# Turning attention outputs and q by DMA transposes instead of by TensorE, in a fused attention and gated-convolution kernel

## The chip, the cores and the metric

One core of a Trainium2 chip. The time is that of one execution on the device, in microseconds, as the median of several executions. "Span" is the stretch from the first to the last instruction in the profiled execution; it is 1.6 to 1.9 us shorter than the time. An execution is called slow when it is over 1.5% above the fastest of its kernel. Slices of a profile are counted from 0.

## The reference, cut to what matters

Block attention whose keys and values are first mixed by a small matrix P per head (five rounds of row and column normalisation), then two dense layers with a depthwise convolution as gate between them. There are 4 batches, 8 heads, 768 positions, head size 64; blocks of 96 positions; model width 512, inner width 1024.

```python
k_sorted = np.einsum('bhij,bhjcd->bhicd', P, k_b)     # v_sorted alike
scores = scale * np.matmul(q_b, k_sb.transpose(0, 1, 2, 4, 3))
attn = softmax(scores);  o = np.matmul(attn, v_sb)
x = o.transpose(0, 2, 1, 3).reshape(B, S, H * D)
h = np.maximum(x @ w_in, 0.0)
out = (h * sigmoid(conv3(h, conv_w))) @ w_out
```

The kernel's matmuls sum over the partitions of both operands (the first dimension of a tile), so q must lie as (head dim, position) before the scores, and the attention output as (model width, position) before the first dense layer. Both have to be transposed, in pieces of 64 or 128 columns. That is what the change is about.

## The kernel before

All work is cut into tokens such as `T.1.3d2` (step T, batch 1, part 3, PSUM slot d2). A long table gives their order, and each engine executes its share of that order, in order. The letters: Q turns q, K and V mix keys and values, S scores, E exponentials, PV attention times values, X normalisation, T turns the output, H first dense layer, C convolution, O second dense layer; a trailing `e` is the copy out of PSUM. Loads (`lk`, `lq`, `lv`, `wout`) are issued by GpSimd, stores by SP.

```python
def turn_q(b, g, slot):                       # 24 transposes: 4 heads of one batch
    ps = psum.tile([128, 2, 1024], BF, name=slot)
    ...
                nc.tensor.transpose(ps[hh * 64:(hh + 1) * 64, e, x * 128:(x + 1) * 128],
                                    qb[b][:, h, x * D:(x + 1) * D], ident, tile_position=(0, hh * 64))

def do_T(b, j, eng, slot):                    # 4 transposes of 96x128
    xn = at.pop(("X", b, j))
    ps = bank(slot, [128, 4, BLK], BF)
    for ii in range(4):
        nc.tensor.transpose(ps[:, ii, :], xn[:, ii].rearrange("c h d -> c (h d)"), ident[0:BLK, 0:BLK])
    at[("T", b, j)] = ps

def do_Te(b, j, eng, slot):                   # copy to SBUF, permuted to position order
    ...
    copy_to(eng, xT[(b, s)][:, hp].rearrange("p (x i t) -> p x i t", x=NX, i=4),
            at.pop(("T", b, j)).rearrange("p i (x t) -> p x i t", x=NX))
```

The softmax here doesn't subtract the row's maximum and nothing guards it: scores larger than these inputs give would overflow.

## Time and profile before

| | before |
|---|---|
| time, median of 3 | 178.76 us (178.65 to 184.08) |
| TensorE busy | 162.9 us of 176.1 |
| VectorE (DVE), ScalarE (ACT) busy | 118.4 and 116.7 us |
| granted TensorE clock | 0.999 |
| input loads under way | until about 64 us |

The prediction below shows and reads the page.

### The profile page before, as it was taken

The numbers are of one execution on the slowest core, as the hardware profiler recorded it, in microseconds if no ns is written. First come the engines' busy times: TensorE is split into PE (matmuls) and PEld (weight loads), VectorE is DVE, ScalarE is ACT, GpSimd is POOL, SyncE is SP. The second block draws the span as 40 slices with busy tenths as digits, with TensorE's granted clock in tenths as the row PEclk, the third lists the DMA queues.
The fourth block names the chain that finished last, engine by engine and source line by source line (L and its number), as shares of the span: only waits on it lengthen the run. The fifth ranks groups of instructions, "written<-read, shape, count | busy, mean of one in ns | idle before, by whom it ended". The sixth has DMA issues, their size and how long they took to land.

```text
span 176.1 us, 6511 instructions
## 1 busy us (share of the span) xinstructions
PE 162.9 (92%) x2907; PEld 106.9 (61%) x2918; DVE 118.4 (67%) x224; ACT 116.7 (66%) x210; POOL 42.0 (24%) x96
## 2 busy tenths in 40 slices
PE   3997989998889999999999999999999999999991
...
DMA  3994799999999960000113322110001000131443
GB/s 48 200 212 89 113 219 217 196 220 209 215 200 218 203 110 4 0 7 0 63 60 120 121 92 90 62 61 4 2 4 60 6 0 0 63 119 60 180 181 119
DMA packets 10688, 18.27 MB, mean 104 GB/s; under 512 B 908, under 2 KB 6052, under 8 KB 10660
## 3 DMA queue, kind: packets, MB, share of 16 engines
...
## 4 chain that ended last, share of the span: by engine, by line
PE 69%; ACT 13%; DVE 10%; issue 3%; DMA 3%; DVEq 0%; ACTq 0%
PE D L502 22%; PE D L447 22%; PE D L467 9%; ACT et L402 4%; PE D L413 4%; PE D L333 3%; PE D L367 3%; DVE hE L457 3%; PE D L430 2%; ACT kT L102 2%; ACT hE L455 2%; DMA sn<-in_sort_net_dram 2%; PE D L394 2%; PE D L230 2%; ACT sg L486 2%
## 5 line engine op out<-in xcount | busy, mean ns | idle before, releaser
L447 PE MATMUL D<-xT,w_in_bf 128*128 128x384 bf16 x256 | 46.3, 326 | 0.8 <-DVE hE L457 0.5
L502 PE MATMUL D<-w_out_bf,hg 128*128 128x512 bf16 x181 | 42.7, 379 | 0.6 <-issue 0.2
L447 PEld LDWEIGHTS <-w_in_bf 128*128 128x128 bf16 x256 | 23.6, 98 | 15.4 <-issue 1.3
L495 DVE SCALAR_TENSOR_TENSOR hg<-sg,hE 128x768 bf16<-128x768 bf16 x32 | 30.8, 981 | 2.7 <-ACT sg L486 2.5
L486 ACT ACTIVATE sg<-D 64x384 bf16<-64x384 f32 x64 | 31.1, 486 | 0.8
L502 PEld LDWEIGHTS <-hg 128*128 128x128 bf16 x192 | 17.8, 98 | 20.6 <-issue 0.8
L354 POOL COPY rv<-vr 128x384 bf16<-128x384 bf16 x24 | 20.9, 910 | 36.6 <-PE D L367 25.6
L402 ACT ACTIVATE et<-D 128x768 bf16<-128x768 f32 x32 | 24.3, 820 | 6.6 <-PE D L394 6.6
L457 DVE TENSOR_SCALAR hE<-D 128x384 bf16<-128x384 f32 x29 | 15.7, 554 | 16.2 <-ACT hE L455 9.7
L455 ACT ACTIVATE hE<-D 128x384 bf16<-128x384 f32 x35 | 16.1, 491 | 14.6 <-PE D L447 7.7
L422 DVE TENSOR_TENSOR xn<-D,rc 96x512 bf16<-96x512 f32 x32 | 22.0, 687 | 1.1
L467 PE MATMUL D<-hE,dg 64*64 64x384 bf16 (+2 forms) x512 | 19.6, 286 | 0.7 <-PE D L394 0.5
L484 ACT ACTIVATE sg<-D 128x384 bf16<-128x384 f32 x32 | 15.8, 492 | 4.2 <-PE D L467 3.4
L106 DVE COPY o_sb<-D 128x512 f32<-128x512 f32 x13 | 8.9, 692 | 13.6 <-PE D L502 11.0
L467 PEld LDWEIGHTS <-dg 64*64 64x64 bf16 x512 | 12.5, 106 | 6.6 <-issue 3.6
L102 ACT COPY o_sb<-D 128x512 f32<-128x512 f32 x11 | 6.4, 587 | 13.8 <-PE D L502 13.7
L413 PE MATMUL D<-vE,et 128*128 128x65 bf16 x256 | 13.2, 194 | 0.8 <-ACT hE L455 0.5
L413 PEld LDWEIGHTS <-et 128*128 128x128 bf16 x256 | 10.6, 98 | 4.2 <-issue 2.2
L102 ACT CAST kT<-D 128x1024 bf16<-128x1024 f32 x10 | 9.9, 1013 | 3.5 <-PE D L333 3.3
L394 PE MATMUL D<-qT,kT 64*128 64x96 bf16 x256 | 9.5, 204 | 1.2 <-DVE qT L106 0.3
L420 DVE RECIPROCAL rc<-D 96x8 f32<-96x8 f32 x32 | 6.3, 198 | 6.0 <-PE D L413 5.9
L430 PE MATMUL D<-ident,xn 96*128 96x96 bf16 x128 | 9.9, 206 | 0.3
...
## 6 DMA issues: line engine op xcount, KB each, us to landing
...
qb<-in_q_dram POOLq DMA_DIRECT2D x3, 768.0 KB, 18.5
...
sn<-in_sort_net_dram SPq DMA_DIRECT2D x1, 8.0 KB, 3.2
```

The lines of the kernel that those rows point to most:

```text
L102: nc.scalar.copy(dst, src)
L354: nc.gpsimd.tensor_copy(rv[:, n * 8:(n + 1) * 8, 0:CC], vr[b].rearrange("p c d -> p d c")[:, n * 8:(n + 1) * 8, :])
L402: nc.scalar.activation(et[:, 0:8 * BLK].rearrange("c (h q) -> c h q", h=2), at.pop(("S", b, j))[:, :, 0:4 * BLK], AF.Exp, scale=scale)
L413: nc.tensor.matmul(pov[:, hh, ii, :], lhsT=et[:, o:o + 128], rhs=vE[b % 2][:, (hh * HP + hp) * NB + sub * 4 + ii, 0:65], start=True, stop= ...
L422: nc.vector.tensor_mul(xn.rearrange("c i h d -> c h i d"), pov[0:BLK, :, :, 0:64], rc.unsqueeze(3).to_broadcast((BLK, 2, 4, D)))
L447: nc.tensor.matmul(ph[:, n, 0:384], lhsT=w_in_bf[:, kc, f * 128:(f + 1) * 128], rhs=xT[(b, s)][:, kc, :], start=(kc == 0), stop=(kc == KC ...
L455: nc.scalar.activation(hv, src, AF.Relu, scale=0.5)
L457: nc.vector.tensor_scalar(hv, in0=src, scalar1=0.0, scalar2=0.5, op0=OP.max, op1=OP.mult)
L467: nc.tensor.matmul(pu[o:o + 64, n, (x0 - 3 * n) * 128:(x0 - 3 * n + nx) * 128], lhsT=dg[64 * i:64 * (i + 1), tap, f, :], rhs=src[64 * i:64 ...
L486: nc.scalar.activation(sg[o:o + 64, 384:768], pu[64 - o:128 - o, 1, 0:384], AF.Tanh)
L495: nc.vector.scalar_tensor_tensor(out=hg.rearrange("p (x c) -> p x c", c=128), in0=sg.rearrange("p (x c) -> p x c", c=128), scalar=1.0, in1 ...
L502: nc.tensor.matmul(po, lhsT=hgs[(b, f)][:, x * 128:(x + 1) * 128], rhs=w_out_bf[:, f, :], start=(f == 0), stop=(f == FC - 1))
```

## The change

The intent: take 192 of the transposes, and the copies behind them, off TensorE, ACT and DVE, and let the DMA crossbar write the turned data straight into SBUF. The outputs of batches 1 to 3 (24 transposes of 96x512, token `T.b.js`) and q of batches 2 and 3 (4 transposes of 128x1536, token `Q.b.gs`, after a copy `Qc` on DVE that puts head pairs side by side) are issued by SP. The order table is a new one (not repeated here). The cut below, with gaps marked, also leaves out the new layouts of q and of the turned outputs in SBUF.

```diff
-NET, NHE, NSG, NXN, NOS = 6, 12, 6, 4, 6
+NET, NHE, NSG, NXN, NOS = 6, 12, 6, 8, 6
 ...
-        qb[b] = rows.tile([128, H, NX * D], BF, name="qb")
+        qb[b] = rows.tile([128, H, NX * D], BF, name="qb", bufs=1)
 ...
 def do_Q(b, g, eng, slot):
-    at[("Q", b, g)] = turn_q(b, g, slot)
+    if b < 2:
+        at[("Q", b, g)] = turn_q(b, g, slot)
+        return
+    qTs[(b, g)] = att.tile([128, NX, 2, 128], BF, name=f"qT{(2 * b + g) % 4}", bufs=1)
+    nc.sync.dma_start(out=qTs[(b, g)].rearrange("p x e t -> p (x e) t"), in_=at.pop(("Qc", b, g)), transpose=True)
+def do_Qc(b, g, eng, slot):
+    qp = rows.tile([128, NX, 4, D], BF, name="qp")
+    nc.vector.tensor_copy(qp, qb[b][:, 4 * g:4 * g + 4].rearrange("p h (x d) -> p x h d", d=D))
 ...
 def do_T(b, j, eng, slot):
     xn = at.pop(("X", b, j))
+    if eng == "S":
+        nc.sync.dma_start(out=xt_part(b, j), in_=xn.rearrange("c i h d -> c (i h d)"), transpose=True)
+        return
 ...
 def do_H(b, p, s, eng, slot):
-                             rhs=xT[(b, s)][:, kc, :], ...
+                             rhs=xT[(b, s)][:, kc].rearrange("p i (x t) -> p x i t", t=PB), ...
```

More of the change, by code (lines that the diff above doesn't have):

```diff
@@ L13 @@
 AX = mybir.AxisListType
-NET, NHE, NSG, NXN, NOS = 6, 12, 6, 4, 6
+NET, NHE, NSG, NXN, NOS = 6, 12, 6, 8, 6
 SUBS = [(hp, s) for s in range(2) for hp in range(4)]
 ORDER = """
-Q.0.1d0 K.0.2d1 K.0.1d2 Qe.0.1d Ke.0.2a M.0.2d1 M.0.1d0 win.0 M.0.0d3 Ke.0.1d lk.1 bdm.0d2 Me.0.2a Me.0.0a K.0.0d1
-lv.1 lq.1 lk.2 Ke.0.0a Me.0.1d lv.2 bdv.0 V.0.0d0 V.0.1d2 S.0.0d3 S.0.1d1 dg.0.2 Ve.0.0d E.0.0 Ve.0.1d V.0.3d0
-S.0.2d2 E.0.1 V.0.2d3 E.0.2 S.0.3d1 Ve.0.3d S.0.5d0 bd.1 Ve.0.2d bd.3 E.0.3 PV.0.0d3 X.0.0 E.0.5 S.0.6d2 PV.0.1d1
@@ L24 @@
-S.0.7d0 X.0.1 PV.0.2d3 lq.2 E.0.6 T.0.0d2 S.0.4d1 E.0.7 Te.0.0a PV.0.3d0 E.0.4 X.0.2 T.0.1d3 bd.2 PV.0.5d2 Te.0.1a
-T.0.2d1 X.0.3 Te.0.2d T.0.3d0 Te.0.3d PV.0.4d3 X.0.5 PV.0.6d1 H.0.0.0d0 R.1.7 H.0.2.0d2 X.0.4 K.1.1d3 He.0.1.0a
-He.0.0.0d He.0.5.0d He.0.4.0a K.1.2d0 Ke.1.2a X.0.6 Ke.1.1d K.1.0d2 H.0.3.0d1 lk.3 T.0.4d3 Ke.1.0a R.1.1 R.1.6
-T.0.5d0 Te.0.4d PV.0.7d2 R.1.0 He.0.7.0d H.0.1.0d3 He.0.6.0a R.1.2 R.1.3 X.0.7 dg.0.1 T.0.6d1 Te.0.5d He.0.2.0a
-He.0.3.0d Te.0.6d V.1.3d2 V.1.0d0 Ve.1.0a Q.1.1d1 Ve.1.3d Q.1.0d3 lq.3 R.1.5 T.0.7d0 Qe.1.1d Te.0.7a S.1.3d1 Qe.1.0d
@@ L29 @@
-E.1.3 S.1.2d2 dg.0.0 S.1.0d3 E.1.2 S.1.1d0 H.0.2.1d1 S.1.5d2 E.1.1 V.1.1d0 R.1.4 E.1.0 He.0.5.1d He.0.4.1d E.1.5
-Ve.1.1d S.1.4d3 C.0.5d1 V.1.2d2 R.2.1 E.1.4 K.2.1d0 Ce.0.5 Ve.1.2d H.0.1.1d3 R.2.7 PV.1.3d2 Ge.0.5 PV.1.1d1 Ke.2.1a
-X.1.3 He.0.2.1a R.2.0 X.1.1 C.0.2d0 R.2.3 He.0.3.1a H.0.0.1d3 PV.1.0d1 Ce.0.2 T.1.3d2 He.0.0.1d X.1.0 He.0.1.1a
-S.1.7d0 PV.1.2d3 Te.1.3a C.0.1d2 E.1.7 T.1.0d1 Ce.0.1 PV.1.7d0 Te.1.0a X.1.2 H.0.3.1d3 X.1.7 He.0.7.1d He.0.6.1a
-T.1.2d0 Te.1.2d S.1.6d2 E.1.6 Ge.0.1 C.0.3d1 T.1.1d3 PV.1.5d0 Q.2.0d2 Te.1.1a X.1.5 R.2.2 R.2.6 K.2.2d3 Ce.0.3
@@ L34 @@
-Ke.2.2a Q.2.1d0 Qe.2.0d C.0.0d1 C.0.7d2 PV.1.6d3 Qe.2.1d Ce.0.0 H.1.0.0d0 X.1.6 Ce.0.7 T.1.7d1 Te.1.7a H.1.1.0d3
-He.1.0.0d Q.3.1d2 Q.3.0d1 Ge.0.2 He.1.2.0a He.1.3.0a Ge.0.3 He.1.1.0a Qe.3.1d K.2.0d3 T.1.6d0 R.2.5 Ge.0.0 Ke.2.0a
-lv.3 R.2.4 H.1.3.0d2 He.1.7.0a PV.1.4d3 He.1.6.0a Te.1.6d V.2.2d0 Qe.3.0d C.0.4d1 T.1.5d2 X.1.4 H.1.2.0d3 Ve.2.2d
-Ce.0.4 T.1.4d0 Te.1.5d S.2.1d2 C.0.6d1 He.1.4.0d He.1.5.0a S.2.3d3 E.2.1 Te.1.4d K.3.1d0 Ge.0.7 Ce.0.6 E.2.3 wout.0
-H.1.2.1d2 Ke.3.1d S.2.0d1 S.2.2d0 He.1.5.1d E.2.0 H.1.0.1d3 E.2.2 K.3.0d1 He.1.1.1a He.1.4.1d Ge.0.6 He.1.0.1d
@@ L39 @@
-V.2.0d0 V.2.3d3 Ke.3.0a C.1.4d2 Ve.2.3a Ge.0.4 Ce.1.4 Ve.2.0d H.1.1.1d1 K.3.2d3 He.1.3.1a He.1.2.1d V.2.1d0 S.2.4d2
-H.1.3.1d1 Ke.3.2d He.1.7.1d C.1.1d3 E.2.4 Ve.2.1a He.1.6.1a Ce.1.1 C.1.0d2 PV.2.3d0 Ge.1.4 O.0.4d1 Ce.1.0 C.1.5d3
-X.2.3 C.1.3d0 Oe.0.4d Ce.1.5 PV.2.1d1 R.3.5 O.0.1d2 C.1.2d3 Ge.1.1 Ce.1.3 Ce.1.2 X.2.1 Oe.0.1d Ge.1.5 C.1.7d1
-PV.2.0d2 O.0.3d0 X.2.0 O.0.2d2 Ge.1.2 Ce.1.7 Oe.0.3d S.2.5d0 R.3.2 E.2.5 Ge.1.0 S.3.1d1 R.3.4 R.3.3 Oe.0.2d C.1.6d3
-E.3.1 O.0.0d2 Ge.1.3 Ce.1.6 T.2.3d1 Ge.1.7 O.0.5d0 Oe.0.0d R.3.7 Ge.1.6 Te.2.3a PV.2.2d1 R.3.1 T.2.0d2 Oe.0.5a X.2.2
@@ L44 @@
-Te.2.0a O.1.0d3 T.2.1d1 T.2.2d2 V.3.1d0 Oe.1.0a Te.2.2d R.3.0 S.2.7d3 S.2.6d2 Te.2.1a Ve.3.1a O.1.2d1 R.3.6 E.2.6
-O.1.3d0 Oe.1.2d PV.2.4d1 E.2.7 Oe.1.3a V.3.2d3 Ve.3.2a X.2.4 V.3.3d2 PV.2.6d0 X.2.6 H.2.1.0d1 T.2.4d3 Te.2.4d
-Ve.3.3a PV.2.5d0 S.3.4d2 X.2.5 He.2.3.0a V.3.0d3 He.2.2.0a Ve.3.0d S.3.0d1 E.3.4 PV.2.7d0 E.3.0 O.1.5d2 T.2.6d3
-T.2.5d1 X.2.7 Oe.1.5d H.2.0.0d0 Te.2.5d S.3.3d1 S.3.2d2 E.3.2 Te.2.6d O.1.1d3 E.3.3 He.2.0.0a He.2.1.0d T.2.7d2
-Te.2.7d PV.3.0d1 Oe.1.1a S.3.6d0 X.3.0 E.3.6 PV.3.1d2 H.2.1.1d3 S.3.5d0 S.3.7d1 X.3.1 PV.3.3d2 He.2.3.1a E.3.5
@@ L49 @@
-He.2.2.1d H.2.2.1d3 X.3.3 PV.3.2d2 T.3.1d0 E.3.7 H.2.2.0d1 He.2.5.1a X.3.2 Te.3.1a T.3.2d2 He.2.4.1d Te.3.2d T.3.0d0
-C.2.3d3 Te.3.0d PV.3.6d2 T.3.3d0 X.3.6 He.2.5.0a He.2.4.0a Te.3.3d H.2.0.1d1 Ce.2.3 T.3.6d2 He.2.1.1a PV.3.7d0
-He.2.0.1d C.2.5d3 Te.3.6a X.3.7 C.2.2d1 PV.3.5d2 Ce.2.5 H.2.3.0d0 X.3.5 He.2.6.0d C.2.0d2 He.2.7.0d Ce.2.2 C.2.1d3
-PV.3.4d1 Ce.2.0 Ge.2.3 Ge.2.2 O.1.4d0 H.3.1.0d2 X.3.4 Ce.2.1 Oe.1.4a T.3.4d3 T.3.7d0 Ge.2.0 Te.3.4d He.3.3.0d
-He.3.2.0a H.3.0.0d1 H.2.3.1d2 T.3.5d3 Te.3.7d Ge.2.1 He.3.1.0a Te.3.5d H.3.2.0d0 C.2.4d3 He.3.0.0d He.2.6.1a
@@ L54 @@
-He.2.7.1d He.3.4.0d C.2.6d2 He.3.5.0d Ce.2.4 C.2.7d1 H.3.3.1d0 Ce.2.6 H.3.0.1d3 H.3.3.0d2 Ce.2.7 H.3.1.1d1 Ge.2.5
-He.3.7.1d He.3.0.1a He.3.1.1d Ge.2.4 He.3.6.1a He.3.6.0a He.3.7.0a He.3.2.1a Ge.2.7 He.3.3.1a H.3.2.1d0 Ge.2.6
-C.3.1d1 C.3.2d2 O.2.4d3 He.3.5.1a Ce.3.1 Ce.3.2 C.3.3d1 He.3.4.1d C.3.0d0 Oe.2.4a C.3.5d2 O.2.3d3 Ge.3.1 Ge.3.2
-Ce.3.3 Oe.2.3d O.2.0d1 Ce.3.0 Ce.3.5 C.3.4d3 C.3.7d0 Ge.3.0 Ce.3.4 Oe.2.0d C.3.6d2 Ge.3.3 Ge.3.4 Ce.3.6 O.2.2d1
-Ge.3.5 Ge.3.6 Ce.3.7 Ge.3.7 O.2.5d3 O.2.1d2 Oe.2.5a O.3.1d3 Oe.2.1d O.3.4d2 Oe.2.2a O.3.0d1 O.3.5d0 Oe.3.1d O.3.3d3
@@ L59 @@
-Oe.3.4d Oe.3.0a Oe.3.5a O.3.2d0 Oe.3.3d Oe.3.2a
+Q.0.1d0 K.0.2d1 K.0.1d2 M.0.1d3 Ke.0.1d Ke.0.2a K.0.0d2 Qe.0.1a Me.0.1d win.0 M.0.2d1 M.0.0d0 lv.1 Ke.0.0a Me.0.2a
+S.0.0d3 lq.1 lk.1 Me.0.0d S.0.1d1 lk.2 V.0.2d2 lv.2 E.0.0 S.0.3d3 V.0.3d0 E.0.1 V.0.0d1 Ve.0.2d bdm.0d2 E.0.3
+Ve.0.3a Ve.0.0d V.0.1d3 S.0.2d1 E.0.2 S.0.4d0 E.0.4 Ve.0.1d bdv.0 PV.0.0d3 S.0.6d1 PV.0.3d2 E.0.6 X.0.0 S.0.5d0
+X.0.3 R.1.2 PV.0.2d3 R.1.7 PV.0.1d1 X.0.2 E.0.5 R.1.3 bd.1 T.0.0d2 Te.0.0a S.0.7d0 PV.0.4d3 T.0.2d2 R.1.6 E.0.7
@@ new lines @@
+X.0.1 T.0.1d1 PV.0.5d0 Te.0.2a X.0.4 X.0.5 R.1.1 PV.0.6d2 Te.0.1a T.0.3d3 Te.0.3a PV.0.7d1 T.0.4d0 X.0.6 R.1.5 R.1.4
+X.0.7 H.0.1.0d3 T.0.5d2 T.0.6d1 Te.0.4a V.1.1d0 He.0.3.0d He.0.2.0d Te.0.5a T.0.7d3 Te.0.6a Te.0.7a V.1.3d1 Q.1.0d2
+Ve.1.1d bd.2 Q.1.1d0 dg.0.0 Ve.1.3a V.1.2d1 H.0.2.0d3 Qe.1.1a Ve.1.2a He.0.5.0a H.0.1.1d0 He.0.4.0d Qe.1.0d R.1.0
+K.1.0d3 lq.2 He.0.3.1d He.0.2.1a K.1.1d2 Ke.1.1d V.1.0d0 Ke.1.0a K.1.2d1 Ke.1.2d H.0.0.1d2 S.1.2d1 Ve.1.0a E.1.2
+lk.3 S.1.1d0 H.0.2.1d3 S.1.0d1 dg.0.1 He.0.1.1d dg.0.2 He.0.5.1d He.0.0.1a E.1.1 S.1.3d0 R.2.4 E.1.0 He.0.4.1d
@@ new lines @@
+PV.1.1d2 C.0.3d3 E.1.3 PV.1.0d1 X.1.1 Ce.0.3 X.1.0 K.2.0d2 S.1.7d0 C.0.2d1 Ke.2.0d E.1.7 S.1.5d3 Ge.0.3 bd.3
+PV.1.3d2 R.2.0 E.1.5 H.0.0.0d0 PV.1.5d3 Ce.0.2 X.1.3 Qc.2.1 He.0.1.0a He.0.0.0a R.2.7 X.1.5 R.2.2 H.0.3.0d2 T.1.1s
+T.1.3s R.2.1 He.0.7.0d S.1.4d0 C.0.0d1 T.1.5s Qc.2.0 R.2.3 He.0.6.0a PV.1.2d2 Ge.0.2 H.0.3.1d3 R.2.5 E.1.4 Ce.0.0
+C.0.1d0 X.1.2 He.0.6.1d R.2.6 PV.1.7d2 K.2.1d1 He.0.7.1a Ce.0.1 K.2.2d3 X.1.7 Ke.2.1d Q.2.1s V.2.1d2 S.1.6d0 T.1.0s
+Q.2.0s C.0.5d1 Ke.2.2a E.1.6 V.2.2d3 Ve.2.1d PV.1.4d2 T.1.2s Ge.0.1 V.2.0d0 lq.3 Ce.0.5 X.1.4 lv.3 T.1.7s Ve.2.2a
@@ new lines @@
+K.3.1d1 Ke.3.1a PV.1.6d2 Ve.2.0d S.2.3d3 wout.0 E.2.3 S.2.0d0 X.1.6 V.2.3d1 S.2.1d2 E.2.0 E.2.1 Ge.0.0 C.0.7d3
+H.1.2.0d0 C.0.6d2 T.1.6s Ve.2.3d C.0.4d1 Ce.0.7 He.1.5.0d He.1.4.0a PV.2.0d3 H.1.0.0d0 T.1.4s Ce.0.6 R.3.3 Ge.0.5
+PV.2.1d2 Ce.0.4 X.2.0 He.1.0.0a H.1.1.1d3 R.3.6 He.1.1.0a R.3.1 X.2.1 K.3.0d2 T.2.0s He.1.2.1a He.1.3.1d S.2.5d0
+E.2.5 Ke.3.0d S.2.2d1 E.2.2 H.1.0.1d3 R.3.5 S.2.6d2 S.2.4d0 S.2.7d1 T.2.1s He.1.1.1d He.1.0.1a Ge.0.4 Qc.3.0
+H.1.1.0d3 E.2.6 E.2.4 E.2.7 R.3.0 PV.2.3d2 R.3.7 K.3.2d0 He.1.2.0a PV.2.6d1 He.1.3.0d C.1.0d3 X.2.3 Ke.3.2a Ce.1.0
@@ new lines @@
+C.1.3d2 PV.2.7d0 X.2.6 R.3.4 H.1.3.1d1 X.2.7 R.3.2 Ce.1.3 He.1.6.1d PV.2.5d3 He.1.7.1a X.2.5 H.1.3.0d0 PV.2.4d2
+V.3.3d3 V.3.0d1 He.1.7.0a Q.3.0s He.1.6.0a V.3.2d0 X.2.4 Ge.0.7 Ge.0.6 Ve.3.3a H.1.2.1d2 PV.2.2d3 Ve.3.0a X.2.2
+O.0.0d1 He.1.5.1a Oe.0.0d S.3.1d3 Ve.3.2a He.1.4.1a E.3.1 S.3.4d0 V.3.1d2 E.3.4 C.1.5d1 O.0.3d3 T.2.4s Ge.1.0
+Ve.3.1d Qc.3.1 S.3.0d2 C.1.4d0 Ce.1.5 C.1.1d1 E.3.0 T.2.7s T.2.6s Ce.1.4 PV.3.0d2 T.2.2s Oe.0.3d O.0.2d3 PV.3.1d0
+Ce.1.1 X.3.0 T.2.3s Ge.1.3 Q.3.1s O.0.5d2 X.3.1 Oe.0.2a C.1.2d0 S.3.6d3 Oe.0.5a Ce.1.2 PV.3.4d1 Ge.1.4 O.0.1d2 E.3.6
@@ new lines @@
+Ge.1.5 X.3.4 S.3.7d1 S.3.2d0 E.3.7 H.2.0.0d3 Oe.0.1d S.3.3d1 S.3.5d2 E.3.2 He.2.0.0a Ge.1.1 C.1.7d0 E.3.3 He.2.1.0d
+T.2.5s C.1.6d3 H.2.1.0d1 E.3.5 Ce.1.6 Ce.1.7 H.2.0.1d2 Ge.1.2 T.3.1s H.2.1.1d3 He.2.3.0a He.2.0.1d He.2.1.1d
+PV.3.5d0 H.2.2.0d2 He.2.2.0d T.3.0s He.2.2.1a X.3.5 H.2.2.1d1 T.3.5s He.2.4.0d PV.3.7d0 T.3.4s Ge.1.7 Ge.1.6
+He.2.3.1a He.2.5.0a He.2.5.1d He.2.4.1a O.0.4d2 Oe.0.4a C.2.0d1 C.2.1d3 PV.3.2d2 X.3.7 X.3.2 Ce.2.0 O.1.2d0 C.2.3d2
+Ce.2.1 C.2.4d1 Ce.2.3 Oe.1.2d PV.3.3d0 O.1.0d3 X.3.3 T.3.2s H.2.3.1d0 Ce.2.4 Ge.2.1 H.2.3.0d1 Ge.2.3 Oe.1.0a
@@ new lines @@
+He.2.6.1a PV.3.6d3 He.2.7.0a He.2.7.1d Ge.2.0 He.2.6.0d T.3.3s O.1.5d0 C.2.2d1 Oe.1.5a C.2.6d2 Ce.2.2 C.2.5d0 Ce.2.6
+T.3.7s X.3.6 H.3.1.0d3 Ce.2.5 He.3.3.0a H.3.2.0d1 He.3.2.0a Ge.2.2 H.3.0.0d2 T.3.6s H.3.0.1d0 He.3.5.0a He.3.1.0a
+He.3.0.0d He.3.4.0a H.3.3.1d3 H.3.2.1d1 Ge.2.5 He.3.4.1d H.3.1.1d2 He.3.0.1d He.3.5.1a C.2.7d1 He.3.1.1a He.3.7.1a
+He.3.3.1a C.3.0d0 He.3.2.1d Ce.2.7 He.3.6.1d Ge.2.6 C.3.3d2 O.1.3d3 Ce.3.0 Ce.3.3 O.1.4d1 Ge.2.4 O.1.1d0 Oe.1.3d
+Ge.2.7 C.3.4d2 C.3.2d3 Oe.1.4d Ce.3.4 C.3.1d1 Oe.1.1d O.2.3d0 Ce.3.1 H.3.3.0d2 Ge.3.3 Ce.3.2 O.2.2d1 O.2.0d3 Oe.2.3d
@@ L60 @@
+He.3.6.0d Ge.3.0 C.3.6d0 Oe.2.2a C.3.5d1 Ge.3.1 Ge.3.4 He.3.7.0a Oe.2.0a Ge.3.2 Ce.3.6 Ge.3.6 C.3.7d3 Ce.3.7 Ge.3.7
+O.2.1d2 Ce.3.5 O.2.5d0 O.2.4d3 Ge.3.5 Oe.2.1a O.3.5d2 Oe.2.4a O.3.0d3 O.3.1d1 Oe.2.5d O.3.4d0 Oe.3.5a O.3.2d2
+Oe.3.4d O.3.3d0 Oe.3.1a Oe.3.0a Oe.3.3a Oe.3.2d
 """
@@ L243 @@
             keep(WARM[3], cws[:, 0, 0:2])
-            t = att.tile([128, 2, NX, 128], BF, name="qT0", bufs=1)
-            nc.scalar.copy(t.rearrange("p e x t -> p e (x t)"), ps[:, :, 0:S])
-            for e in range(2):
-                qTs[(0, e)] = t[:, e]
+            qTs[(0, 0)] = att.tile([128, NX, 2, 128], BF, name="qT0", bufs=1)
+            nc.scalar.copy(qTs[(0, 0)].rearrange("p x e t -> p e x t"),
+                           ps[:, :, 0:S].rearrange("p e (x t) -> p e x t", t=128))
         nc.vector.reduce_sum(out=rs, in_=sn[:, 0:NB, :], axis=AX.X)
@@ L379, in do_Q @@
     def do_Q(b, g, eng, slot):
-        at[("Q", b, g)] = turn_q(b, g, slot)
+        if b < 2:
[6 more added lines that the diff above has]
+        nc.vector.tensor_copy(qp, qb[b][:, 4 * g:4 * g + 4].rearrange("p h (x d) -> p x h d", d=D))
+        at[("Qc", b, g)] = qp.rearrange("p x h d -> p (x h d)")
     def do_Qe(b, g, eng, slot):
-        t = att.tile([128, 2, NX, 128], BF, name=f"qT{(2 * b + g) % 4}", bufs=1)
-        copy_to(eng, t.rearrange("p e x t -> p e (x t)"), at.pop(("Q", b, g))[:, :, 0:S])
-        for e in range(2):
-            qTs[(b, 2 * g + e)] = t[:, e]
+        ps = at.pop(("Q", b, g))
+        qTs[(b, g)] = att.tile([128, NX, 2, 128], BF, name=f"qT{(2 * b + g) % 4}", bufs=1)
+        copy_to(eng, qTs[(b, g)].rearrange("p x e t -> p e x t"),
+                ps[:, :, 0:S].rearrange("p e (x t) -> p e x t", t=128))
     def do_S(b, j, eng, slot):
@@ L395, in do_S @@
                                  lhsT=kT[b % 2][hh * 64:(hh + 1) * 64, hp * NB + i].rearrange("p a c -> p (a c)"),
-                                 rhs=qTs[(b, hp)][hh * 64:(hh + 1) * 64, :, i * PB:(i + 1) * PB],
+                                 rhs=qTs[(b, hp // 2)][hh * 64:(hh + 1) * 64, :, hp % 2, i * PB:(i + 1) * PB],
                                  start=True, stop=True)
@@ L418, in do_X @@
         pov = at.pop(("PV", b, j))
-        rc = att.tile([BLK, 2, 4], FP, name=f"rc{j % NXN}", bufs=1)
+        rc = att.tile([BLK, 2, 4], FP, name=f"rc{(8 * b + j) % NXN}", bufs=1)
         nc.vector.reciprocal(rc, pov[0:BLK, :, :, 64])
-        xn = att.tile([BLK, 4, 2, D], BF, name=f"xn{j % NXN}", bufs=1)
+        xn = att.tile([BLK, 4, 2, D], BF, name=f"xn{(8 * b + j) % NXN}", bufs=1)
         nc.vector.tensor_mul(xn.rearrange("c i h d -> c h i d"), pov[0:BLK, :, :, 0:64],
@@ L424, in do_X, with xt_part @@
         at[("X", b, j)] = xn
+    xT = {}
+    def xt_part(b, j):
+        hp, s = SUBS[j]
+        if (b, s) not in xT:
+            xT[(b, s)] = moep.tile([128, KC, 4, BLK], BF, name=f"xT{(2 * b + s) % 4}", bufs=1)
+        return xT[(b, s)][:, hp]
     def do_T(b, j, eng, slot):
         xn = at.pop(("X", b, j))
+        if eng == "S":
+            nc.sync.dma_start(out=xt_part(b, j), in_=xn.rearrange("c i h d -> c (i h d)"), transpose=True)
+            return
         ps = bank(slot, [128, 4, BLK], BF)
```

11 lines of the change are left out of this document (3 added, 8 removed).

## The prediction

> **What bounds the kernel now.** I read the page's busy shares first, then the slices, then who waited for whom on TensorE, then the chain of waits piece by piece.
>
> ```profile
> span 176.1 us, 6511 instructions
> PE 162.9 (92%) x2907; PEld 106.9 (61%) x2918; DVE 118.4 (67%) x224; ACT 116.7 (66%) x210; POOL 42.0 (24%) x96
> PE   3997989998889999999999999999999999999991
> DMA  3994799999999960000113322110001000131443
> PE 69%; ACT 13%; DVE 10%; issue 3%; DMA 3%; DVEq 0%; ACTq 0%
> ```
>
> TensorE is busy in nearly every slice after the start; no other engine passes 67%. The DMA engines are saturated only until about 63 us (slice 14) and nearly idle after, apart from the output stores. The chain of waits is 69% TensorE. That TensorE hardly waits is told by the longest waits of that engine:
>
> ```profile
> PE D L218 <- POOL ident L151: 3.0, 1, 3.0
> PE D L333 <- ACT kT L102: 0.6, 1, 0.6
> PE D L447 <- DVE hE L457: 0.5, 2, 0.4
> PE D L467 <- PE D L394: 0.5, 1, 0.5
> ```
>
> The 3.0 us belong to the start; no later releaser costs more than 0.6 us. So between about 15.4 us (first key mixing) and 172.2 us (end of the last output matmul) the kernel is a nearly full TensorE queue, and what is taken from that queue should come off the end. The time itself is a few us over the span (177.84 against 176.1 us in the profiled execution), and I assume this offset stays.
>
> What a transpose really costs the queue is not its mean duration, as durations overlap. The rows say
>
> ```profile
> L430 PE MATMUL D<-ident,xn 96*128 96x96 bf16 x128 | 9.9, 206 | 0.3
> L230 PE MATMUL D<-ident,qb 128*64 128x128 bf16 x192 | 6.5, 220 | 0.1
> L106 DVE COPY xT<-D 128x384 bf16<-128x384 bf16 x20 | 6.9, 351 | 4.5 <-PE D L430 4.4
> L102 ACT COPY xT<-D 128x384 bf16<-128x384 bf16 x12 | 5.9, 493 | 0.7 <-PE D L430 0.6
> L106 DVE COPY qT<-D 128x1536 bf16<-128x1536 bf16 x7 | 6.6, 954 | 0.3 <-PE D L230 0.2
> L245 ACT COPY qT<-D 128x1536 bf16<-128x1536 bf16 x1 | 1.4, 1439 | 0.1
> ```
>
> but the chain of waits in order of time, where pieces abut, gives the cost in the queue:
>
> ```profile
> 63.13 1.46 PE D L230 x48
> ...
> 100.47 0.34 PE D L430 x8
> ...
> 134.38 1.30 PE D L447 x8
> ```
>
> 48 q transposes take 1.46 us, 30 ns each; 8 transposes of attention output take 0.34 us, 42 ns each; 8 matmuls of the first dense layer take 1.30 us, 163 ns each.
>
> **What the Trainium skill says.** (1) "TensorE: Matmul & The Clock Gate", Part 4: PE-mode transpose, has a full transpose put in PSUM, with an engine copy after it, and about 275 ns in one kernel's context. The trace agrees on the copy (the xT and qT rows above) and is near in duration (206 and 220 ns), but the queue pays only 42 and 30 ns, and these I use. (2) "VectorE: DVE Perf Modes", The three transpose paths, gives the crossbar 1309 ns for a 128x128 bf16 block, into SBUF. No transfer of the kernel before shows it. (3) "DMA: Bandwidth & Descriptors", Issuing engines are not separate DMA queues: whoever issues, the same 16 DMA engines do the work and interleave. So transposes issued from SP meet the loads issued from POOL; the saturated DMA slices until 63 us agree that there would be no spare room there. (4) "SBUF — State Buffer", Door 1, speaks of 16-byte lines at which consecutive accesses keep full bandwidth; the new read pattern of the first dense layer has runs of 16 bf16, 32 bytes, so it should be free. No row of before shows exactly that case: the score matmuls read q in such runs, but are too small to prove it.
>
> **The change part by part.**
>
> Attention outputs of batches 1 to 3: 24 of the 32 groups of four transposes leave TensorE. 24 x 4 x 42 ns = 4.1 us of TensorE queue, on the path. With them go 24 copies out of PSUM. Batch 0 keeps its eight, all on ACT.
>
> q of batches 2 and 3: four groups of 24 transposes leave. 96 x 30 ns = 2.9 us of TensorE queue, on the path. Four copies of 1536 columns go; in their place come four SBUF copies on DVE that put head pairs side by side. A copy of the same size from PSUM is 954 ns, so I take at most that.
>
> Engines beside it. DVE: minus 20 x 0.351 = 7.0, minus 6 x 0.954 = 5.7, plus at most 4 x 0.95 = 3.8: about 9 us less of 118. ACT: xT copies from 12 to 8 (-2.0 us), q copies from 1 to 3 (+2.9 us): 1 us more of 117. Both at 66% or so: off the path except at short crossings.
>
> PSUM: 28 fewer uses of the four double banks that everything shares (D0 to D3), which helps the order table somewhat.
>
> The dense layer's right operand is now read as (position, block, 16) instead of a flat row: I count 0. The q buffer goes from two to one: the load of batch 2's q must wait until TensorE has turned batch 1's. In the new table that load is listed after 20 us of TensorE work, and q of batch 2 is copied after another 10 us; a q load of before took a median 18.5 us to land under full DMA load. DVE's in-order queue could wait here; it is tight, not clearly broken.
>
> Sum of TensorE: I multiplied the chain's pieces by the tokens of each table (first layer 1.30 us, output group 1.73, gate convolution 0.55, values 0.25, scores 0.28, mixings 0.62, transposes 0.17 a group, q 0.73). Before: 147.4 us of work in the 156.8 us from 15.4 to 172.2, so 9.4 us are gaps. After: 140.4 us. If gaps stay, the time is 178.76 - 7.0 = 171.8 us.
>
> What is given back. SP issues everything in order: 24 output transposes, 4 q transposes, 24 stores. I summed the TensorE work that the new table puts between a transpose's input and its first reader. Mostly it is wide: 6 to 29 us. The narrow places: batch 2's q, where SP has an output transpose of batch 1, q of group 1, an output transpose, and q of group 0 to do in about 7 to 8 us of TensorE work before scores need them, followed by four more transposes that the first dense layer of batch 1 needs within 2 to 6 us; and the last output transpose of batch 3 (3.9 us from its normalisation to its reader). An output transpose is 96x512, 3 blocks of 128x128 in size; as the skill's block is mostly fixed cost, I estimate 2 to 4 us from issue to landing, and 4 to 6 us for q's 128x1536. The first narrow place then just fits or costs 1 to 4 us, the last one 0 to 1. A little comes back from fewer PSUM uses. Net I take 1.3 us off the gain: 173.1 us.
>
> **The rivals.**
>
> A. The wait for the copy becomes a longer wait for the crossbar. For it: SP's queue is serial, the tokens are packed around batch 2's q, and a transpose has a longer latency than a TensorE transpose plus copy (0.2 + 0.4 us). Against it: after 63 us the DMA is nearly empty, and the table is a new one, so surely made with such latencies in mind. If each transpose takes 5 us or SP holds 3 us for each, it gives 176 to 182 us.
>
> B. The transposes collide with the loads. In the table the loads of batch 3's q and v and of the second weights stand exactly beside batch 1's last transposes. Before, 768 KB loads took 14 to 18 us to land while the queue was full. Batch 1's outputs might then come some us late: 174 to 178 us.
>
> C. The dense layer slows because of its runs of 16. If each of the 256 matmuls went from 163 to 200 ns it would be 9.5 us more, and the whole gain would be gone: about 181 us. I give it 5%.
>
> D. DVE or ACT become the bound and the removed work turns into gaps. Against it: DVE falls, ACT hardly moves, both have a third of their time free. In the stretch from 40 to 60 us ACT is at 88% and TensorE at 91%, so there the saving may be half lost: up to 1 us.
>
> **Range and chances.** 171.8 is the arithmetic, 173.1 with the give-back. The lower end, 169.5, has the gaps shrinking by two us too, thanks to freer banks and DVE; the upper end, 178.0, is rival A or B in earnest. The 2% border is 175.2 us, two us above my number. Since the stage that gains is TensorE bound over 150 us and the work plainly leaves it, I put faster at 0.67, same at 0.22, slower at 0.11.
>
> **What would show it.** Right: TensorE's matmul count falls by 192, the rows of transposes go to 32 (xn) and 96 (qb), DVE falls by some 9 us, the spacing of the dense layer stays near 163 ns, and no TensorE wait on a DMA exceeds 1 us. Wrong: waits of TensorE on the DMA of qT or xT that sum to 4 us or more (A, B), landing times of transposes over 5 us, or a dense-layer run of 8 that takes clearly over 1.30 us (C).

## More of the kernel before

The columns are the stretch, its length, then busy us and number of instructions of PE, PEld, DVE, ACT and POOL, the granted TensorE clock, the DMA engines' busy share and GB/s.

```profile
60.00:68.00 8.00, 8.00 (x176) 5.96 (x176) 7.12 (x12) 6.12 (x13) 0.32 (x1) 1.00 0.62 104
68.00:76.00 8.00, 7.80 (x165) 5.22 (x162) 6.23 (x10) 6.76 (x13) 0.52 (x1) 1.00 0.02 4
76.00:81.00 5.00, 4.79 (x158) 3.55 (x151) 3.27 (x5) 4.21 (x7) 0.88 (x2) 1.00 0.02 3
```

TensorE is full, its clock is full, and between 68 and 81 us the DMA engines rest.

## The result, and the profile after

| | before | after |
|---|---|---|
| time, median of 3 | 178.76 us | 199.77 us (198.08 to 200.83) |
| ratio of the fast runs | | 1.117 (95% interval 1.098 to 1.135) |
| TensorE, DVE, ACT busy | 162.9, 118.4, 116.7 us | 162.7, 109.4, 118.2 us |
| granted TensorE clock | 0.999 | 0.934 |

A ratio here is the mean time of one kernel's fast runs over that of the other's fast runs of the same rounds, so it is not quite the ratio of the medians. The change makes the kernel 12% slower. The page of after, at the lines that answer to those of before:

```profile
PE 162.7 (82%) x2726; PEld 102.5 (52%) x2726; DVE 109.4 (55%) x200; ACT 118.2 (60%) x210; POOL 40.2 (20%) x96
PE   3998788997897401799799965999999789999991
PEclk9999999999999655579999996999999999999997
DMA  4992999999439999502400445311422101230434
PE 49%; DMA 18%; ACT 9%; DVE 8%; POOL 6%; issue 6%; SPq 2%; POOLq 0%; ACTq 0%
```

There is a hole in TensorE in slices 13 to 16 (about 64 to 84 us) and its clock falls to half in and after it. Just there the DMA engines are full. The chain of waits, 69% TensorE before, has 18% DMA in it. TensorE's waits between 50 and 100 us (what waited, on what, us in total, times, longest):

```profile
PE D L400 <- DMA qT<-qp: 11.4, 2, 6.9
PE D L364 <- issue: 3.0, 1, 3.0
```

Batch 2's scores wait 11.4 us for the turned q. Another 3.0 us come between two matmuls of one group for which the profile shows nothing that is waited for ("issue"). SP's queue shows why q is late (start, us that SP was held, instruction):

```profile
56.95 3.13 SPq L381 DMA_TRANSPOSE qT<-qp  x1
60.13 3.06 SPq L443 DMA_TRANSPOSE xT<-xn  x1
63.23 12.54 SPq L381 DMA_TRANSPOSE qT<-qp  x1
...
95.44 1.44 SPq L381 DMA_TRANSPOSE qT<-qp  x1
```

The same instruction holds SP 1.44 us at 95 us and 12.54 us at 63 us, and the two q transposes of batch 2 landed 18.3 and 17.1 us after issue. GpSimd had issued the loads of batch 3's q, its v and the second weights at 56.6, 57.6 and 58.1 us. Here the single q buffer takes part: GpSimd had stood 4.5 us until the copy of batch 2's q freed it, and the same copy feeds the second q transpose, so loads and transposes start together. (Before, with two buffers, this load of q went out at 40.2 us; no run gave the second buffer back.) By stretch, with the columns of before:

```profile
60.00:68.00 8.00, 4.91 (x181) 4.27 (x175) 4.96 (x7) 4.80 (x9) 0.00 (x0) 0.88 1.27 169
68.00:76.00 8.00, 0.94 (x16) 0.56 (x13) 2.05 (x4) 0.99 (x2) 0.82 (x1) 0.50 1.23 168
76.00:81.00 5.00, 0.64 (x16) 0.50 (x18) 0.00 (x0) 0.84 (x2) 0.00 (x0) 0.50 1.23 203
```

Before, TensorE is busy 20.6 us of these 21; after, 6.5. That is 14 us of the 21 that the kernel lost. After the hole the clock is still half: one group of the first dense layer (8 matmuls, 1.46 us elsewhere in the same view) takes 2.74 us at 83 us.

### The profile page after: what moved, and what is told of

The parts are those of the page before. It is cut to its first block, busy times and chain, and to the rows that moved or that the text cites. A ratio compares the mean times of both kernels' runs of the same rounds, so it can differ in the third digit from the quotient of the medians.

```text
span 198.1 us, 6184 instructions
## 1 busy us (share of the span) xinstructions
PE 162.7 (82%) x2726; PEld 102.5 (52%) x2726; DVE 109.4 (55%) x200; ACT 118.2 (60%) x210; POOL 40.2 (20%) x96
## 4 chain that ended last, share of the span: by engine, by line
PE 49%; DMA 18%; ACT 9%; DVE 8%; POOL 6%; issue 6%; SPq 2%; POOLq 0%; ACTq 0%
PE D L513 21%; PE D L458 14%; DMA qT<-qp 10%; PE D L478 6%; DMA vr<-in_v_dram 6%; ACT hE L466 3%; PE D L364 3%; DVE hE L468 3%; PE D L419 3%; ACT et L408 2%; PE D L400 2%; DMA xT<-xn 2%; DVE hg L506 2%; DVE xn L428 1%; SPq L443 1%
## 5 line engine op out<-in xcount | busy, mean ns | idle before, releaser
L513 PE MATMUL D<-w_out_bf,hg 128*128 128x512 bf16 x192 | 44.8, 387 | 0.0
L468 DVE TENSOR_SCALAR hE<-D 128x384 bf16<-128x384 f32 x28 | 15.0, 555 | 25.3 <-ACT hE L466 13.4
L351 POOL COPY rv<-vr 128x384 bf16<-128x384 bf16 x24 | 19.2, 840 | 30.8 <-DMA vr<-in_v_dram 22.5
L400 PE MATMUL D<-qT,kT 64*128 64x96 bf16 x256 | 10.3, 212 | 17.2 <-DMA qT<-qp 14.9
L478 PE MATMUL D<-hE,dg 64*64 64x384 bf16 (+2 forms) x512 | 20.6, 294 | 1.4 <-DVE hE L468 1.0
L400 PEld LDWEIGHTS <-kT 64*128 64x128 bf16 x256 | 6.9, 98 | 21.8 <-DMA qT<-qp 15.6
L478 PEld LDWEIGHTS <-dg 64*64 64x64 bf16 x512 | 13.1, 108 | 8.5 <-issue 5.3
L104 DVE COPY o_sb<-D 128x512 f32<-128x512 f32 x11 | 7.6, 691 | 15.5 <-PE D L513 15.5
L100 ACT COPY o_sb<-D 128x512 f32<-128x512 f32 x13 | 7.5, 586 | 13.7 <-PE D L513 10.8
L104 DVE CAST vE<-D 128x1024 bf16<-128x1024 f32 x5 | 6.1, 1220 | 15.1 <-PE D L364 15.1
```

Source lines behind the costliest of these rows:

```text
L351: nc.gpsimd.tensor_copy(rv[:, n * 8:(n + 1) * 8, 0:CC], vr[b].rearrange("p c d -> p d c")[:, n * 8:(n + 1) * 8, :])
L400: nc.tensor.matmul(ps[:, hh, ii * BLK:(ii + 1) * BLK], lhsT=kT[b % 2][hh * 64:(hh + 1) * 64, hp * NB + i].rearrange("p a c -> p (a c)"), r ...
L468: nc.vector.tensor_scalar(hv, in0=src, scalar1=0.0, scalar2=0.5, op0=OP.max, op1=OP.mult)
L478: nc.tensor.matmul(pu[o:o + 64, n, (x0 - 3 * n) * 128:(x0 - 3 * n + nx) * 128], lhsT=dg[64 * i:64 * (i + 1), tap, f, :], rhs=src[64 * i:64 ...
L513: nc.tensor.matmul(po, lhsT=hgs[(b, f)][:, x * 128:(x + 1) * 128], rhs=w_out_bf[:, f, :], start=(f == 0), stop=(f == FC - 1))
```

## The experiments

Four theories. **A**: transposes that meet input loads in the DMA engines take many times as long, and TensorE waits. **B**: the new order table has gaps of its own. **C**: the transposes hold one another up in SP's queue, loads or not. **D**, formed later: the same loads stop TensorE between instructions that wait for no data.

### 1. Loads later

The three loads, and a read that holds them back, move behind batch 1's last output transpose.

```diff
-... Q.2.0s ... V.2.0d0 lq.3 Ce.0.5 X.1.4 lv.3 T.1.7s ... wout.0 ... T.1.4s
+... Q.2.0s ... V.2.0d0 Ce.0.5 X.1.4 T.1.7s ... T.1.4s hold.1 lq.3 lv.3 wout.0
+nc.gpsimd.tensor_copy(held, xT[(1, 1)][:, 0, 0, 0:1])     # do_hold
```

> The changed kernel with one edit: the loads of batch 3's q and v and of the second weights wait until batch 1's last transpose (T.1.4) has landed. Theory A (transposes that meet loads in the DMA engines take many times as long, and TensorE waits for batch 2's q): both q transposes of batch 2 land in under 5 us, TensorE's waits on qT fall from 14.9 us to under 5 (the one of batch 3's second half stays), the granted clock stays near 1.0 around 70 to 80 us, time 178 to 186 us. Theory C (transposes hold one another up in SP's queue, loads or not): q of batch 2 still lands after 10 us or more, waits on qT of 10 us or more, 192 to 200 us. Theory B (the new order table is what costs): waits on qT fall, but the time stays above 192.

Measured: 190.57 us median, ratio 1.045. Batch 2's q landed 3.7 and 4.3 us after issue and its waits are gone. The wait of 3.6 us for batch 3's second q half stays, and a new one of 4.7 us for v's rearranged rows appears, as v now arrives late. So C fails for batch 2's q, A holds for it; the time (fast runs 187.4 and 188.2 us) is above the 178 to 186 that A gave, as I had swapped one late transfer for another.

### 2 to 4. One part at a time in the new table

In the second run only the outputs go through the crossbar, in the third only q, in the fourth nothing. The tokens that return to TensorE get PSUM slots by hand:

```diff
-Qc.2.1 ... Q.2.1s            (2 and 4)
+Q.2.1d1 ... Qe.2.1a
-T.1.4s                       (3 and 4)
+T.1.4d3 ... Te.1.4d
```

> Only the attention outputs go through the crossbar; q of batches 2 and 3 is turned by TensorE and copied, in the new order table (its eight tokens given banks by hand). A: batch 1's outputs still meet the loads, so some wait of TensorE on xT of 2 to 6 us appears, but the 14.9 us on qT are gone: 182 to 190 us. C: output transposes alone are light for SP's queue: 178 to 184. B: above 192.

> Only q of batches 2 and 3 goes through the crossbar; all attention outputs are turned by TensorE and copied, in the new order table. A: batch 2's q still meets the loads and lands after 8 us or more: waits on qT of 6 us or more, 188 to 200 us. C: with no output transposes in SP's queue, q lands in about 4 us and the waits on qT fall below 4 us: 180 to 186. B: above 192 with no such waits.

> The new order table with nothing on the crossbar: all 24 output and 4 q transposes back on TensorE, with banks given by hand. A and C: no DMA waits of TensorE in the middle, 178 to 187 us (some loss for banks that the table wasn't made for). B: above 190 us.

Measured: 193.79 us (ratio 1.069), 201.16 us (1.107) and 205.48 us (1.141). The second and fourth missed the ranges of A, the third lies at its edge (fast runs 197.6 and 200.3 us, 188 to 200 expected), and all three lie about where B was expected (above 192, above 192 without waits on q, above 190); the fourth is slower than the full change, the third about as slow. But the profiles show waits that my slots made: in the third and fourth 4.8 us of transposes on ACT's tanh reads that still held the slot, in the second and fourth 1.5 us on q's copies. So they do not tell the table from the crossbar, and I draw nothing from the times of 3 and 4. Two readings of the traces remain. In the second (its profile just counts as slow) TensorE waits once for 7.1 us on an output transpose (landing 9.8 us at the most, 2.4 in the median), while the three loads, issued at 66.9 to 68.4 us, run: A for the small transposes too. In the third, batch 2's q went out before the loads (51.9 and 54.7 us, loads from 55.0), landed after 4.5 and 7.8 us, and the wait that A expected did not come; but TensorE stops for 2.7 and 1.9 us put down to issue, with only loads running.

### 5. The disputed cost by itself

The kernel before, with four transposes added that nobody reads, one in flight at a time:

```diff
+zq = att.tile([128, 12, 128], BF, name="z", bufs=1)
+nc.sync.dma_start(out=zq, in_=w_in_bf.rearrange("p k f -> p (k f)")[:, b * 1536:(b + 1) * 1536], transpose=True)
+# and 96x512; the first pair as soon as w_in has landed, the second after batch 0's first stores
```

> The kernel before, unchanged in its work, with four extra transposes whose results nobody reads, one in flight at a time: one of the output's shape (96x512) and one of q's (128x1536) while the input loads run (about 27 us), the same two at about 90 us when no load runs. It measures the disputed cost without any other transpose in flight and in the old order table. A (loads): about 1.2 and 1.4 us of SP's time and 2 to 4 us to landing at 90 us, but at 27 us at least three times as long for q's shape, 8 us or more. C (transposes hold up one another): the pair at 27 us takes about what the pair at 90 us takes. The kernel's time stays within 2 us of before under both.

SP's queue in that run, first 96x512 (L293) and 128x1536 (L290) beside the loads, then the same pair without:

```profile
25.88 1.26 SPq L293 DMA_TRANSPOSE z<-w_in_bf  x1
35.78 8.56 SPq L290 DMA_TRANSPOSE z<-w_in_bf  x1
...
93.06 1.20 SPq L293 DMA_TRANSPOSE z<-w_in_bf  x1
...
96.33 1.50 SPq L290 DMA_TRANSPOSE z<-w_in_bf  x1
```

And from issue to landing, in the windows around the first, the second, and the last two:

```profile
DMA to landing us min/median/max: 9.9/9.9/9.9
...
DMA to landing us min/median/max: 21.8/21.8/21.8
...
DMA to landing us min/median/max: 2.3/3.7/5.2
```

The small shape takes 9.9 us beside loads and 2.3 without, the large one 21.8 and 5.2 (the last beside a store). No other transpose was in flight and the order table is the old one, so the loads alone do it (one reading of each), and C falls as the reason for the long landings. The kernel's time, 180.95 us against 180.57, hardly moved, since nobody waited for these four.

### 6 and 7. Loads in the gap, and batch 3's second half earlier

```diff
 6: -lk.3 ...  Q.2.0s ... lq.3 ... lv.3 ... wout.0
    +lk.3 lv.3 ...  Q.2.0s hold.2 lq.3 wout.0            # hold.2 reads qT(2, 0)
 7: as 6, and
    -Q.3.0s ... Qc.3.1 ... T.2.7s T.2.6s T.2.2s ... Oe.0.3d ... T.2.3s ... Q.3.1s
    +Q.3.0s Qc.3.1 Q.3.1s ... T.2.7s T.2.6s T.2.2s ... Oe.0.3d ... T.2.3s
```

> The changed kernel with the three loads moved apart: batch 3's v right after batch 3's k (in the gap that the loads leave), batch 3's q and the second weights only once batch 2's q has been turned (instead of after batch 1's last output transpose as in the run with the loads later). A: both q transposes of batch 2 land in under 5 us, no TensorE wait on v's rearranged rows over 1 us (4.7 us in the run with the loads later), the wait on batch 3's second q half of 3.6 us stays: 179 to 186 us. If batch 1's last output transposes now meet the loads, a wait on xT of 3 us or more shows, 184 to 190. B (the order table costs by itself): above 186 without such waits.

> The run before it with a second edit: batch 3's second q half is copied and turned right after its first half, ahead of nine output transposes and a store in SP's queue. If SP's order is what makes TensorE wait 3.6 us there, this wait and the fall of the clock after it go: 3 to 5 us less than the run before it, 174 to 182 us. If the copy on DVE or the buffer is what comes late, the wait stays and the time is the same within 1 us.

Run 6: 190.65 us, ratio 1.058. Batch 2's q landed after 4.6 and 5.1 us and v's wait is gone, but now TensorE waits 5.2 us for an output transpose of batch 1 that met the two loads, and 3.6 us for batch 3's second half, with the clock falling to 0.5 or 0.6 after each. It missed its first range and is what its second sentence described, with a time at or just above the 190 us given there. Run 7: 184.25 us, ratio 1.011 (0.999 to 1.024; fast runs 182.29 and 181.98). The wait for batch 3's second half is gone: it had waited in SP's queue behind output transposes and a store, not for its data. The fast runs gain 8 us on run 6, more than the 3 to 5 expected, but not by this repair alone: the 5.2 us for an output transpose are gone too, and TensorE waits 2.8 us for batch 2's second q half, which landed after 5.7 us among transposes, with no load running.

### 8 and 9. The old order table, with only those transposes that meet no load

Run 8 keeps the old table and puts only the outputs of batches 2 and 3 on the crossbar. Run 9 adds q of batch 3, issued at 72 us.

```diff
 8: -X.2.3 ... T.2.3d1 ... Te.2.3a            (all 16 of batches 2 and 3)
    +X.2.3 T.2.3s
 9: -Q.3.1d2 Q.3.0d1 ... Qe.3.1d ... Qe.3.0d
    +Te.1.4d Qc.3.1 Q.3.1s ... Qc.3.0 Q.3.0s S.2.0d1   # qp: one buffer, NXN = 6
```

> The old order table with only the output transposes of batches 2 and 3 on the crossbar, each issued right after its normalisation, and the new layout of xT; batches 0 and 1 and all of q stay on TensorE. All loads are done by then and the old table leaves 4.5 us of TensorE work or more between normalisation and reader. 64 transposes of 42 ns are 2.7 us less in TensorE's queue. A: transposes land in 2 to 4 us, no TensorE wait on them, 174.5 to 178 us, ratio to before 0.98 to 0.995. If the gaps just grow by what is taken out, ratio 0.995 to 1.005. If SP's order (stores behind transposes) costs, above 1.005.

> The old order table with the output transposes of batches 2 and 3 (as in the run before of that kind) and also q of batch 3 on the crossbar, both issued after the loads have ended; everything else on TensorE. TensorE's queue loses 64 x 42 ns + 48 x 30 ns = 4.1 us. A (only transposes beside loads hurt): no TensorE wait on a transpose, ratio to before 0.975 to 0.985, 174.5 to 177 us. If gaps grow by what is taken out: 0.99 to 1.005.

Run 8: 178.43 us against 180.57, ratio 0.990 (0.972 to 1.007), so unclear by itself. Run 9, in five rounds: 178.07 us against 181.96, ratio 0.987 (0.980 to 0.994). That is the best correct version found: its interval lies below 1. Its transposes landed in 2.3 to 5.0 us, none is waited for over 0.4 us, and the granted clock is 0.996. Of the 4.1 us that leave TensorE's queue about 2.3 arrive at the end (1.3% of 180.3, the mean of the fast runs of before): new waits of 1.5 us on DVE and 1.0 us on ACT take part of it.

### 10. All transposes, with everything learnt so far

```diff
 as 7, but: lk.3 lv.3 wout.0 together; lq.3 held until T.1.4s has landed;
-X.1.3 Qc.2.1 ... T.1.1s T.1.3s ... T.1.5s Qc.2.0 ... Q.2.1s ... T.1.0s Q.2.0s
+X.1.3 Qc.2.1 Q.2.1s Qc.2.0 Q.2.0s ... T.1.1s T.1.3s ... T.1.5s ... T.1.0s
```

> The changed kernel with its own order table and the whole set of transposes, but: batch 3's v and the second weights load right after batch 3's k, only batch 3's q waits until batch 1's last output transpose has landed; batch 2's q is copied and turned before batch 1's output transposes in SP's queue instead of after three of them, and batch 3's second half right after its first. A (loads and the place in SP's queue are the whole loss): no TensorE wait on qT or xT over 1.5 us, no fall of the clock, 173 to 179 us, ratio 0.965 to 1.0. B (the order table costs by itself too): waits gone, but 180 us or more.

184.17 us, ratio 1.020. No wait on q is left, but one of 2.6 us on an output transpose is, since all ten of batch 1 and early batch 2 now queue in SP behind the two of q (7.9 us, beside the second weights' load), and there are stops put down to issue of 1.6 and 0.7 us. A did not get its range; B had gained ground. The larger stop matters below:

```profile
64.54 0.44 PE L367 MATMUL D<-bd,rv 128*64 128x64 bf16 x15
66.59 0.47 PE L367 MATMUL D<-bd,rv 128*64 128x64 bf16 x17 [1.61 <-issue]
```

By then the loads had ended: from 62 to 71 us GpSimd's queue, which carries them, shows no packet, and SP's transposes fill the DMA engines until 64 us.

### 11 and 12. The order table with transposes that cost nothing

Wrong results on purpose: later batches read batch 0's turned data. In 11 no crossbar transpose is issued; in 12 all are, into tiles that nobody reads.

```diff
-nc.sync.dma_start(out=qTs[(b, g)]..., in_=at.pop(("Qc", b, g)), transpose=True)
+qTs[(b, g)] = qTs[(0, g)]                       # 11; in 12 the DMA goes to a sink
-nc.sync.dma_start(out=xt_part(b, j), in_=..., transpose=True)
+xT[(b, SUBS[j][1])] = xT[(0, SUBS[j][1])]
```

> Wrong results on purpose: the changed kernel with its order table, but the 28 crossbar transposes are not issued at all; scores and the first dense layer of the later batches read batch 0's q and outputs, which lie there already, so nothing waits for a transpose. The loads keep their place. It is the order table with transposes that cost nothing. A (waits for transposes are the whole loss): the arithmetic of the prediction comes true, 170 to 175 us, clock near 1.0. B (the order table has gaps of its own): 178 us or more.

> Wrong results on purpose: as the run without transposes, but all 28 crossbar transposes are issued, into tiles that nobody reads. TensorE never waits for one; what they still do is use the DMA engines beside the loads and instruction fetches. If only the waiting costs, the time is that of the run without transposes within 1.5 us. If their traffic also holds back loads or instruction fetches, waits on v's rows or stalls put down to issue grow and it is 2 to 6 us above it.

Run 11: 182.45 us, ratio 1.019, where the prediction's arithmetic said 172. Most of TensorE's saving is gone even where a transpose costs nothing. Run 12: 182.39 us in its one fast run, as run 11 (only the waiting costs), but 186.7 to 187.5 in three that count as slow. The trace of 11 shows two stops in the middle of groups:

```profile
61.42 0.44 PE L363 MATMUL D<-bd,rv 128*64 128x64 bf16 x15
64.61 0.61 PE L363 MATMUL D<-bd,rv 128*64 128x64 bf16 x17 [2.75 <-issue]
...
68.55 0.68 PE L477 MATMUL D<-hE,dg 64*64 64x384 bf16 x14
71.17 0.35 PE L477 MATMUL D<-hE,dg 64*64 64x384 bf16 x2 [1.95 <-issue]
```

A group of 32 matmuls stops after 15, one of 16 after 14; the profile shows no data that they wait for. The first is the very place of the 3.0 us stop in the changed kernel (15 and 17 of the same step), and run 12 stops at both. One packet of the DMA queue that the page calls "instruction" runs in the microsecond from 62 and one in that from 68. That gave theory D.

### 13 and 14. Without the late loads

Wrong results on purpose: batch 2's q and v are used again and GpSimd fills the second weights.

```diff
-load_w(w_out_bf, moe_w_out, 128)
+nc.gpsimd.memset(w_out_bf, 0.01)
-load_v(b)                  # b == 3; load_q alike
+vr[3] = vr[2]
```

> Wrong results on purpose: the run without transposes, and also without the loads of batch 3's q and v (batch 2's are used again) and of the second weights (filled by GpSimd instead). If those loads hold back TensorE's instructions (theory D), the stops of 2.8 and 1.9 us put down to issue shrink below 0.5 us each, the clock stays at 1.0 and the time falls to 171 to 176 us. If the order table has gaps of its own (theory B), the time stays at 179 us or more.

> Wrong results on purpose: the changed kernel with all its transposes and its order table, without the loads of batch 3's q and v and of the second weights. A with D (the meeting of transposes, instruction fetches and loads is nearly the whole loss, beside SP's queue at batch 3's second q half): q of batch 2 lands in under 5 us, no stops put down to issue above 1 us, the wait of 3.5 us for batch 3's second q half stays, 176 to 182 us. If the transposes alone cost what is missing: above 188 us.

Run 13: 177.36 us, ratio 0.989; the stops are gone (the largest put down to issue after 50 us is 0.4) and the clock is 0.995. The same stretch in runs 11 and 13:

```profile
60.00:70.00 10.00, 6.47 (x198) 5.34 (x191) 6.70 (x9) 6.63 (x10) 2.90 (x3) 0.83 1.17 205
...
60.00:70.00 10.00, 9.22 (x304) 7.31 (x303) 8.88 (x13) 9.74 (x16) 3.85 (x5) 1.00 0.02 5
```

The time lies between the range of D (171 to 176 us) and that of B (179 or more). The stops bear D out: with the loads two, without them none. But loads are not the only way to a stop: run 10 stopped 1.6 us (and run 6 0.9 us) at the same 15th matmul with transposes and no load in the DMA engines. Run 14: 182.85 us, ratio 1.016; no q lands later than 5.3 us after issue and no stop is left, but the 3.2 us for batch 3's second half stays with its fall of the clock. Both runs carry a fault of my own: GpSimd's fill ran while DVE copied q, which took 3.17 us in place of 0.55 and made TensorE wait 1.9 us. So 13 is some 2 us too slow.

## Why the prediction was wrong, point by point

Runs 11, 13, 14 and the changed kernel make a square. Medians (of the fast runs where a run had slow ones) and ratios to before:

| | no late loads | late loads |
|---|---|---|
| no crossbar transposes | 177.2 us, 0.989 | 182.5 us, 1.019 |
| crossbar transposes | 182.5 us, 1.016 | 199.8 us, 1.117 |

Loads alone add 0.030 (D), transposes alone 0.027 (SP's order, by the 3.2 us wait of run 14), together 0.128. The meeting itself is the rest, 0.071 or about 12.7 us of 178.8; the four intervals together leave some 0.03 either way. It is the largest part of the loss, and the traces put A behind it: 11.4 us of waits for batch 2's q, which are absent in the other three. (My fault of 2 us is in both runs of the left column: it leaves the 0.071 as it is and makes the loads' share too small by about 0.01.)

- **TensorE is the bound, and the work leaves its queue: right.** Its recorded matmuls went from 2907 to 2726: 192 transposes less, and 11 records of the last layer that the first trace lacked (181 against 192). DVE fell by 9.0 us (I had 9), ACT rose by 1.5 (I had 1). (24 x 4 x 42 ns is 4.0 us, not 4.1; nothing hangs on it.)
- **The first dense layer reads runs of 16 for free: right.** Groups of eight still take 1.30 us in the chain of waits where the clock is full; rival C falls.
- **"If gaps stay, the time is 178.76 - 7.0 = 171.8 us": wrong.** With transposes free and late loads absent the table gives 177.2, or some 175 without my fault. So 3 us of the saving go to gaps that the table has of its own (B, in part; I have not traced them one by one), and 5 us more to the stops of D and the half clock after them, which the prediction did not have at all.
- **"4 to 6 us for q's 128x1536", with "the first narrow place then just fits or costs 1 to 4 us": this is the step that failed most.** The place was the right one. The figure is right for idle DMA engines (3.6 us at the least, 5.2 in the probe) and wrong beside loads, where I used it: 17 and 18 us, for which TensorE waited 11.4 us instead of 1 to 4. I had put the collision under rival B, but for batch 1's outputs only, at "some us"; batch 2's q meets the same loads, as the table lists these right behind it and the single q buffer, which I had weighed for batch 2's load alone, holds them until then.
- **The narrow places: incomplete.** I named two and left out batch 3's second q half, which the new table lists 2.3 us of TensorE work before its reader. It cost 3.5 us of waiting.
- **A wait costs its length: wrong.** After a hole the clock was half for several us more (0.60 from 81 to 88 us). No term of my sum had this.
- **Rival A's size.** It gave 176 to 182 us for transposes of 5 us each. The wait did take the place of the one removed, as rival A said; its length was off by three to four times.

The margin of the range, 178.0 at the upper end, came from treating the two collisions as alternatives of a few us each. They came together and cost more than their sum (the square).

What stays open: why loads delay transposes so much (the traces show it, not the mechanism); what stops TensorE inside a group, since loads do it and in run 10 transposes did, while the kernel before, with loads as dense until 64 us, stopped by no more than 0.2 us (the same stretch in runs 8 and 9 by up to 0.8); and the last 3 us of the order table.

## What to carry to other kernels

A DMA transpose has two prices, one beside loads and one without, and here they differed two-fold (run 10, 7.6 and 8.6 us) to five-fold: measure both, and move only transposes whose stretch is free of loads (run 9: 1.3% gained; the whole set: 12% lost). When work leaves a full TensorE for an asynchronous path, list for each transfer what shares its engines and what stands ahead of it in its issuing queue, not only how much work lies before its reader. And count a hole of some us in TensorE at more than its length: in these traces the clock fell to about half after it and took some us to come back.

## What the Trainium skill lacked or had wrong

- "VectorE: DVE Perf Modes", The three transpose paths, gives 1309 ns for a 128x128 block and no word on shape or load; other pages have bandwidths of transposes, none a time beside loads. Here 96x512 landed in 2.3 us and 128x1536 in 3.6 to 5.2 us on quiet engines, and in 9.9 and 21.8 us beside loads; SP itself is held 1.2 and 1.4 to 1.5 us, and up to 12.5 us beside loads.
- "DMA: Bandwidth & Descriptors", Rules for kernel authors, says that a transpose next to ordinary DMAs needs nothing. It speaks of correct results, and the runs with real data were correct, so this agrees; what it lacks is the cost in time, by the numbers above.
- "Runtime: NRT & Kernel Launch", Instruction fetch mechanics, calls the cost of crossing into the next block of instructions mostly hidden. Beside three loads TensorE stopped 2.75 and 1.95 us in the middle of groups, with a packet of the instruction queue in the same stretch, and without the loads it did not. That the fetch is what stopped it is likely but not shown.
- "TensorE: Matmul & The Clock Gate", Part 1, says that the clock is halved after an idle window of about 3.4 us. In run 11 a stop of 2.75 us was enough, and one of 1.95 us again: after it 8 matmuls of the first dense layer took 2.65 us, 1.46 at full clock. In run 10 the clock stayed full after a stop of 1.6 us and fell to 0.50 after one of 1.3 us (with 0.7 us shortly before), so the length of one stop alone does not decide.
- The same page, Part 4, has about 275 ns for a transpose in a kernel, a duration (206 and 220 ns here), and no cost in the queue, which was 42 and 30 ns.
